# Complex-decay attention before an expert layer: time moves from the free axis to the partitions

## The chip, the cores and the metric

One Trainium2 chip, one of its cores. The metric is the device time of one execution in microseconds (us), from launch to end. A profiled execution of the same program tells where the time goes; it has its own time, given below.

## What is computed

Three layers follow one another: an attention with a complex decay per channel, a mixture of 8 experts where each token goes to one, and a dense layer with a gated nonlinearity. The change is in the first. Its reference, cut to what matters:

```python
mag = np.sqrt(a_re * a_re + a_im * a_im)
scale = np.minimum(mag, 0.999) / (mag + 1e-06)
a_re_n, a_im_n = a_re * scale, a_im * scale
for t in range(S):                       # S = 768 steps, 4 batches, 8 heads, D = 48
    new_re = ar * S_re - ai * S_im
    new_im = ar * S_im + ai * S_re
    kv = np.einsum('bhd,bhe->bhde', k[:, :, t], v[:, :, t])
    S_re, S_im = new_re + kv, new_im
    y[:, :, t] = np.einsum('bhd,bhde->bhe', q[:, :, t], S_re)
```

The kernels don't step through time. They take the logarithm of the decay's size and its angle, sum both along time, and turn them into factors for q and k, so that a chunk of 128 steps becomes matrix products: scores (k by q), a causal mask, scores by v, and a state that is carried from chunk to chunk.

## The kernel before, in words

The attention works on units of one to three chunks of 128 steps of one batch (`UNITS`, 10 units, 24 chunks). All is fp32. In each unit the decays, q and k lie with (head, channel) on the partitions and time along the free axis: 384 channels are 128 partitions by 3 columns of time (`pack`, `row_order`). A unit (`unit`) takes these steps:

- VectorE clamps `ar` (L399), ScalarE takes its logarithm and reciprocal (L400, L401), `ai` is multiplied by the latter (L402), VectorE squares it (L409), ScalarE takes the arctangent (L417).
- **Sums along time** are VectorE scans: the angle (L421, with a carry from the unit before) and the logarithm (L460, begun anew in each chunk). The angle is brought into one turn by L427 (ScalarE) and L431 (VectorE), the last column is kept as the carry (L433).
- ScalarE makes sine, cosine and the growing and falling exponentials; six products of q and k with them follow (`times`, L473), each on VectorE or GpSimd.
- **The move.** The rows of q and k belong to the heads in a packed order, and a matrix product wants one head's real and imaginary part on 112 partitions of one tile `z`. Ten SBUF-to-SBUF transfers per unit on SyncE's queue put them there (`remap`, L348).

A chunk (`chunk`) then has, on TensorE, the scores (L534), two groups of transposes of k (L517), the attended values (L561) and the products for the state (L571); VectorE masks the scores (L542) and carries the state (L575, L581); ScalarE copies what was transposed (L524) and the result `xT` (L600). `Router.steps` follows: a projection (L729), two ScalarE passes (L735, L787) and a score of tiny VectorE instructions (L740 to L814) that route the tokens. When all chunks are done, `Router.blocks` orders the tokens by expert, rows are gathered (`r<-xd`), and the expert layer begins with a transpose (`px`, L1062).

**What sets the order.** Nothing of this order stands in the code as written. `Plan` holds every step as a node with an engine (or a choice of two), a cost in ns, what it reads and writes, and the number of buffers of each tile; `Plan.order` lists them greedily by due time, `Plan.run` tries 600 disturbed due times and emits the best list. It also inserts spare matmuls into TensorE's waits (`busy`, L148). Each engine then runs its list strictly in order. The plan's cost of a scan of 384 columns is 130 + 1.0417 · 384 = 530 ns, and it lets VectorE and GpSimd run side by side at no cost.

Of the kernel before, what the change touches and what calls it, by code (L numbers as in the profile page):

```python
# [69 lines left out]
def const_arrays():  # L70
    t = np.arange(P)
    ca = np.zeros((P, P + W), np.float32)
    ca[:, :P] = t[:, None] <= t[None, :]
    ca[:, P:] = np.arange(W) % P != 0
# [44 lines left out]
def row_order():  # L119

    o = np.zeros((P, NK, 2), np.int64)
    for p in range(96):
        for kc in range(NK):
            o[p, kc] = (2 * kc + p // 48, p % 48)
    for p in range(96, 128):
        o[p, 0] = (6, p - 96)
        o[p, 1] = (7, p - 96)
        o[p, 2] = (6, 32 + p - 96) if p < 112 else (7, 32 + p - 112)
    return o


def slot(h):
    return h if h >= 6 else 3 * (h % 2) + h // 2


def pack(a):

    o = row_order()
    return np.ascontiguousarray(a[:, o[..., 0], :, o[..., 1]].transpose(2, 0, 1, 3))
# [11 lines left out]
class Plan:  # L151

    LAG, OWN, LOAD = 250, 200, 1283
# [8 lines left out]
    def add(s, engs, cost, fn, r=(), w=(), new=(), due=math.inf, table=None, late=0):  # L164
# [4 lines left out]
        n.warm = getattr(fn, "warm", None)  # L169
        n.deps = set()  # L170
# [23 lines left out]
    def order(s, seek, switch, phase=0.0):  # L194
# [4 lines left out]
        ticks = {}  # L199
        opened = {t: [] for t in s.bufs}  # L200
# [39 lines left out]
        while ready:  # L240
            can = []
            low = inf, inf, None
            for n, o in ready.items():
                t = start(n) if n.new else 0
                if t == inf:
                    continue
                due = n.due + switch if n.table and n.table != table else n.due
                for e, cost, r in o:
                    b = max(t, r, free.get(e, 0))
                    can.append((due, n.id, b, e, n, cost))  # L250
                    if (b, due) < low[:2]:
                        low = b, due, e
# [8 lines left out]
            fill, t = 0, b + cost  # L261
            if e == "PE":
# [49 lines left out]
def attention(tc, ctx, cst, ca, qk, v, ar, ai, rt, psr, wkr, chores, last):  # L312

    nc = tc.nc
    N = len(UNITS)
    T = {}
    plan = Plan({"ar": 3, "ai": 3, "t1": 2, "t2": 2, "t3": 2, "qk": 2, "o": 1, "ar_": 1, "ai_": 1, "t1_": 1, "t2_": 2, "t3_": 1,
                 "qk_": 1, "o_": 1, "v": 2, "carry": 2, "kt": 1, "sT": 2, "st": 2, "pt": 2, "ps": 2, "py": 1, "ds": 1, "xT": 1,
                 "pr": 2, "row": 2, "lg": 2, "s": 2, "u": 3, "si": 2, "ws": 9}, free=("t2", "t2_"))
    add = plan.add  # L320
    with ExitStack() as right, ExitStack() as left:
# [4 lines left out]
        wk = left.enter_context(tc.tile_pool(name="a_wk", bufs=2))  # L326
        pst = left.enter_context(tc.tile_pool(name="a_pst", bufs=2, space=PSUM))
# [9 lines left out]
        def packed(k, n, room, top):  # L337

            t = tile_(room, [P, 2 * NK * top * (P + 1)], k)
            T[k] = t[:, :2 * NK * n * (P + 1)].rearrange("p (q k n) -> p q k n", q=2, k=NK)  # L340
            return T[k]

        def remap(z, src, r0):

            for dst, s in ((z[r0:r0 + 48, :, 0:3], src[0:48]), (z[r0:r0 + 48, :, 3:6], src[48:96]),
                           (z[r0:r0 + 32, :, 6:8], src[96:128, :, 0:2]), (z[r0 + 32:r0 + 48, :, 6:7], src[96:112, :, 2:3]),
                           (z[r0 + 32:r0 + 48, :, 7:8], src[112:128, :, 2:3])):
                nc.sync.dma_start(dst.rearrange("p q k n -> p q (k n)"), s.rearrange("p q k n -> p q (k n)"))  # L348

        zs = [zp.tile([DP, 2 * H * (W + U)], F32, tag=f"z{i}", name=f"z{i}") for i in range(2)]  # L350
        cp = left.enter_context(tc.tile_pool(name="a_cst", bufs=1))
        end = left.enter_context(tc.tile_pool(name="a_end", bufs=1))
        a = cp.tile([P, P + W], F32, name="ca")
        caus, begin = a[:, :P], a[:, P:]
        for i in range(2):
            add("Pool", 5200, lambda i=i: nc.gpsimd.memset(zs[i][32:64], 0.0), w=[("z", i, 0), ("z", i, 1)])

        def unit(u):

            b, c0, n = UNITS[u]  # L360
            w = n * P
            e = NK * w
            ts = slice(c0 * P, (c0 + n) * P)
# [3 lines left out]
            AR, AI, T1, T3, QK, O = ((t + mark, u) for t in ("ar", "ai", "t1", "t3", "qk", "o"))  # L367
            TE, TD = ("t2" + mark, 2 * u), ("t2" + mark, 2 * u + 1)
            VV = ("v", u)
            ar3, ai3 = ([(*k, i) for i in range(NK)] for k in (AR, AI))  # L370
# [4 lines left out]
            def x(k):  # L375
                return T[k][:, :, :w]

            def new(k):
                return tile_(room, [P, NK, top * P], k)[:, :, :w]

            def load(k, src):
                def f():
                    nc.sync.dma_start(new(k), src[b, :, :, ts])
                return f

            def loadqk():
                nc.sync.dma_start(packed(QK, n, room, top)[:, :, :, :w], qk[b, :, :, ts].rearrange("p (q k) t -> p q k t", q=2))
# [6 lines left out]
            if u == 0:  # L394
                add("SP", 728, lambda: nc.sync.dma_start(a, ca), w=["ca"], late=2000)
            add("SP", 2.84 * e, loadqk, w=q3 + k3 + [(*QK, "e")], new=[QK], late=2000)
            add("SP", 1.42 * e, loadv, w=[VV], new=[VV], late=2000)

            add("DVE", fast, lambda: V.tensor_scalar(out=x(AR), in0=x(AR), scalar1=1e-5, scalar2=None, op0=ALU.max), w=ar3)  # L399
            add("ACT", actc, lambda: act(x(AR), x(AR), AF.Ln), w=ar3, table=LNEXP)  # L400
            add("ACT", actc, lambda: act(new(T1), x(AR), AF.Exp, scale=-1.0), r=ar3, w=[T1], new=[T1], table=LNEXP)  # L401
            add(both, 0, lambda g: engines[g].tensor_tensor(out=x(AI), in0=x(AI), in1=x(T1), op=ALU.mult), r=[T1], w=ai3)  # L402

            def tan2():
                if n == U:
                    i, o = (T[k].rearrange("p k t -> p (k t)") for k in (AI, T1))
                else:
                    i, o = x(AI), x(T1)
                V.tensor_tensor_reduce(out=o, in0=i, in1=i, scale=1.0, scalar=0.0, op0=ALU.mult, op1=ALU.max,  # L409
                                       accum_out=cst["rmax"][:, u:u + 1])  # L410

            add("DVE", full, tan2, r=ai3, w=[T1, ("rmax", u)])
# [6 lines left out]
            def total(i):  # L419
                def f():  # L420
                    V.tensor_tensor_scan(out=x(AI)[:, i], data0=cst["one"].to_broadcast([P, w]), data1=x(AI)[:, i],  # L421
                                         initial=T["carry", u - 1][:, i:i + 1] if c0 else 0.0, op0=ALU.mult, op1=ALU.add)
                return f

            for i in range(NK):
                add("DVE", 130 + 1.0417 * w, total(i), r=[("carry", u - 1)] if c0 else [], w=[(*AI, i)])
            add("ACT", actc + 94, lambda: act(new(T3).bitcast(I32), x(AI), AF.Identity, scale=1 / (2 * math.pi)),  # L427
                r=ai3, w=[T3], new=[T3])

            def rest():  # L430
                V.scalar_tensor_tensor(out=x(AI), in0=x(T3).bitcast(I32), scalar=-2 * math.pi, in1=x(AI), op0=ALU.mult, op1=ALU.add)  # L431
                if c0 + n < NC:
                    V.tensor_copy(tile_(wk, [P, NK], ("carry", u)), x(AI)[:, :, w - 1])  # L433

            k = [("carry", u)] if c0 + n < NC else []
            add("DVE", full + 200 * len(k), rest, r=[T3], w=ai3 + k, new=k)
# [1228 lines left out]
```

## Time and profile before

| | us |
|---|---|
| median of 3 runs | 986.34 (984.12 to 989.18) |
| profiled execution, its own time | 984.68 |
| its span, first to last instruction | 982.9 |
| TensorE busy | 844.6 (86%) |
| VectorE busy | 665.8 (68%) |
| ScalarE busy | 518.6 (53%) |
| GpSimd busy | 313.1 (32%) |

The shares are means over three layers with different limits. The attention with its routing takes the first third of the span; the two dense layers after it are the same instructions in both kernels. In the profile PE is TensorE's matrix products, PEld its weight loads, DVE VectorE, ACT ScalarE, POOL GpSimd, SP SyncE; a q behind the name is the engine's queue. One fp32 matrix product shows as two PE records, one transpose as one.

### The profile page before, as it was taken

To read this page: it belongs to the slowest core of one execution; us is meant where nothing else is said; L and a number is where in the kernel's file an instruction comes from. 1 tells how busy PE (TensorE), PEld (TensorE's weight loads), DVE (VectorE), ACT (ScalarE), POOL (GpSimd) and SP (SyncE) were. 2 spreads that over 40 slices of the span, in tenths; PEclk is the share of its full clock that TensorE was granted. 3 is DMA by queue.
4 is the path that set the end of the run, shared out by engine and by line. 5 is a ranking of instruction groups with operands and counts; after the bars stand their busy time and mean duration, and the time that the engine had idled before them with its cause. 6 is when DMAs were issued, how large, how long until landed. Compare 5 with 4: busy or idle time off the path is not lost.

```text
span 982.9 us, 17388 instructions
## 1 busy us (share of the span) xinstructions
PE 844.6 (86%) x5994; PEld 561.3 (57%) x5994; DVE 665.8 (68%) x1367; ACT 518.6 (53%) x987; POOL 313.1 (32%) x253
## 2 busy tenths in 40 slices
PE   0567687578786899998899999999999999999994
PEld 0567686568685566655556654444655545556662
DVE  7999998999776799988999659998045071250000
ACT  6756667667655576774773347676054172340000
POOL 7546252634421674451550112331320100001110
PEclk9777787888896999999999999999999999999998
DMA  8589867697674574663656432330110000000000
GB/s 264 147 194 210 147 169 178 110 204 140 123 233 152 163 199 154 197 188 122 181 174 207 149 121 62 93 97 1 49 49 9 25 1 17 17 2 25 27 30 19
DMA packets 58020, 114.15 MB, mean 116 GB/s; under 512 B 7521, under 2 KB 36834, under 8 KB 57922
## 3 DMA queue, kind: packets, MB, share of 16 engines
q1 hardware_dynamic: 52754, 97.02, 37.7%
q0 software_dynamic: 4736, 14.69, 4.9%
q8 instruction: 56, 0.92, 0.4%
q10 hardware_dynamic: 432, 1.18, 0.4%
q14 instruction: 42, 0.34, 0.1%
HBM read 75.04 MB, written 18.81 MB: 95 GB/s over the span
## 4 chain that ended last, share of the span: by engine, by line
PE 45%; DVE 12%; DMA 3%; issue 3%; ACT 3%; POOL 0%; POOLq 0%; DVEq 0%; ACTq 0%
PE fpo L1303 18%; PE fph L1283 11%; PE py L1099 6%; PE ph L1074 4%; PE ph L1075 2%; DVE w L955 2%; DMA wh<-w 2%; DVE x L1287 2%; DVE acc L1106 1%; PE pt L1084 1%; DVE h L1078 1%; DVE hT L1088 1%; PE px L1062 1%; DVE w L958 1%; ACT h L1077 1%
## 5 line engine op out<-in xcount | busy, mean ns | idle before, releaser
L1283 PE MATMUL fph<-fx,fw 128*128 128x512 f16 x864 | 192.2, 379 | 5.6 <-DVE x L1287 5.6
L1287 DVE SCALAR_TENSOR_TENSOR x<-fph,x 128x512 f32<-128x512 f32 x96 | 65.9, 688 | 129.8 <-ACT x L1286 128.2
L1283 PEld LDWEIGHTS <-fw 128*128 128x128 f16 x864 | 84.4, 98 | 104.3 <-issue 8.8
L1303 PE MATMUL fpo<-fw,gT 128*128 128x384 f16 x768 | 125.3, 326 | 0.0
L1099 PE MATMUL py<-w,hT 128*128 x624 | 118.0, 326 | 1.2
L1074 PE MATMUL ph<-w,x 128*128 x312 | 107.5, 379 | 1.8 <-ACT x L1063 0.9
L534 PE MATMUL ps<-z 112*128 112x128 f32 x384 | 68.7, 337 | 44.0 <-DMA z<-qk 37.8
L1303 PEld LDWEIGHTS <-gT 128*128 128x128 f16 x768 | 75.1, 98 | 49.9
L1307 ACT ACTIVATE x<-fpo,fsm 128x384 f32<-128x384 f32 x24 | 13.9, 580 | 167.5 <-PE fpo L1303 167.5
L1308 POOL DMA_INDIRECT out<-x,fto x24 | 23.2, 965 | 245.4 <-ACT x L1307 245.4
L994 POOL TENSOR_TENSOR w<-ws,w 128x768 f16<-128x768 f32 x40 | 68.6, 1716 | 83.3 <-ACT w L993 79.1
L1286 ACT ACTIVATE x<-fph,fsm 128x512 f32<-128x512 f32 x96 | 65.5, 684 | 49.1 <-PE fph L1283 36.2
L534 PEld LDWEIGHTS ps<-z 112*128 112x128 f32 x384 | 60.8, 242 | 49.1 <-DMA z<-qk 27.7
L1075 PE MATMUL ph<-w,x 128*128 x312 | 84.9, 272 | 1.6 <-DVE x L1064 1.5
L1099 PEld LDWEIGHTS <-hT 128*128 128x128 f16 x624 | 60.9, 98 | 32.4 <-issue 3.6
L1077 ACT COPY h<-ph 128x256 f32<-128x256 f32 x104 | 38.4, 369 | 57.0 <-PE ph L1075 50.3
L1303 PE MATMUL fpo<-fw,x 128*128 128x384 f16 x384 | 62.7, 326 | 0.0
L1078 DVE TENSOR_TENSOR h<-ph,h 128x256 f32<-128x256 f32 x104 | 43.5, 418 | 26.9 <-ACT h L1077 21.6
L1303 PEld LDWEIGHTS <-x 128*128 128x128 f16 x384 | 37.6, 98 | 25.0
L561 PE MATMUL py<-z,st 112*48 112x128 f32 (+1 forms) x320 | 38.0, 320 | 13.0 <-DVE st L581 6.6
L1106 DVE SCALAR_TENSOR_TENSOR acc<-py,rs,acc 128x384 f32<-128x384 f32 x78 | 47.6, 610 | 1.4 <-PE pt L1084 0.6
L1074 PEld LDWEIGHTS <-x 128*128 128x128 f16 x312 | 30.5, 98 | 31.0 <-ACT x L1063 1.6
(239 smaller groups left out, 1735.6 us busy)
## 6 DMA issues: line engine op xcount, KB each, us to landing
ws<-in_we SPq DMA_DIRECT2D x61, 384.0 KB
w<-in_w SPq DMA_DIRECT2D x32, 384.0 KB
qk<-in_qk SPq DMA_DIRECT2D x6, 1152.0 KB
z<-o SPq DMA_DIRECT2D x12, 435.4 KB
z<-qk SPq DMA_DIRECT2D x12, 435.4 KB
yd<-acc SPq DMA_DIRECT2D x26, 192.5 KB
xd<-row SPq DMA_DIRECT2D x6, 589.5 KB
ar<-in_ar SPq DMA_DIRECT2D x6, 576.0 KB
```

Of the source, the lines that this page charges most:

```text
L534: nc.tensor.matmul(ps[:, h - 4 * i, :], lhsT=T["z", u][:, 1, slot(h), ts], rhs=T["z", u][:, 0, slot(h), ts], start=True, stop=True)
L994: nc.gpsimd.tensor_tensor(out=wv[:, :, 1, :], in0=sv, in1=wv[:, :, 0, :], op=ALU.subtract)
L1074: nc.tensor.matmul(ph, lhsT=xT[:, b - lo, 0, k, :], rhs=w[:, e, o:o + 2 * FQ], start=k == 0, stop=False)
L1075: nc.tensor.matmul(ph[:, :FQ], lhsT=xT[:, b - lo, 1, k, :], rhs=w[:, e, o:o + FQ], start=False, stop=k == KD - 1)
L1077: nc.scalar.copy(h, ph[:, FQ:])
L1078: nc.vector.tensor_tensor(out=h, in0=ph[:, :FQ], in1=h, op=ALU.add)
L1099: nc.tensor.matmul(py, lhsT=hT[:, hl, j, :], rhs=w[:, e, o + off:o + off + DM], start=i == 0, stop=i == n - 1)
L1106: nc.vector.scalar_tensor_tensor(out=a, in0=py, scalar=s, in1=a, op0=ALU.mult, op1=ALU.add)
L1283: nc.tensor.matmul(ph, lhsT=s.wi[f][:, a, k, :], rhs=xT[b][:, k], start=i == 0, stop=i == 3 * KD - 1)
L1286: nc.scalar.activation(h, ph, AF.Sigmoid, scale=sig)
L1287: nc.vector.scalar_tensor_tensor(out=h, in0=ph, scalar=GS, in1=h, op0=ALU.mult, op1=ALU.mult)
L1303: nc.tensor.matmul(po, lhsT=gT[:, f, a, g * P:(g + 1) * P], rhs=s.wo[f][:, b, :], start=i == 0, stop=i == 3 * s.NF - 1)
```

## The change

Time goes onto the partitions, channels onto the free axis. A chunk of `ar`, `ai`, q, k is a tile of 128 steps by 384 channels (`by_time`), all heads side by side.

- The sums along time are matrix products with a triangle of ones (`caus`): `total` in `phases` (angle, L401, plus L403 which adds the last row of the chunk before by a weight tile that is one on partition 127) and in `logs` (logarithm, L447). They land in PSUM (`sc`, two banks), from where ScalarE and VectorE read, chunk by chunk: L406, L409, L450, L455. The scans, the carry and L433 are gone.
- The products with sine and cosine write one tile `f` (`turn` in `unit`, L491) in which the 48 real and 48 imaginary channels of a head lie side by side. The `z` tiles, their zeroing on GpSimd (L356), `ends` (L479) and `remap` are gone.
- Per chunk, 16 transposes on TensorE (L517: 8 heads, q and k, also in a batch's last chunk, where before there were 8 transposes of k and none in the last chunk) turn `f` into `zq` and `zk`, and four copies of 96x512 bring them from PSUM, on ScalarE or VectorE (L525). The scores (L535) read these. The state's products (L569) read `f` as it lies, 8 instead of 16 per chunk.
- The decay over a chunk, which before was a column, is now a row: two transfers per unit (`whole`, L464), one small transpose (L467) and a copy (L472) turn it.
- The routing tile `pr` has one PSUM buffer instead of two; the scores share three banks with the transposes.
- `Plan` learns of a shared port: a VectorE or GpSimd node marked `port` isn't begun while a marked one of the other engine runs.

The core of the diff:

```diff
+        n.port = port or getattr(fn, "port", False)
...
+        pair = {"DVE": ("Pool", 0), "Pool": ("DVE", 0)}
...
                     b = max(t, r, free.get(e, 0))
+                    if n.port and e in pair and pair[e][1] > b:
+                        b = pair[e][1]
...
+            if n.port and e in pair:
+                pair[pair[e][0]] = e, t
...
-            def total(i):
-                def f():
-                    V.tensor_tensor_scan(out=x(AI)[:, i], data0=cst["one"].to_broadcast([P, w]), data1=x(AI)[:, i],
-                                         initial=T["carry", u - 1][:, i:i + 1] if c0 else 0.0, op0=ALU.mult, op1=ALU.add)
-                return f
...
+                def total():
+                    if j == 0:
+                        new(T3)
+                    ps = tile_(psc, [P, 512], S)[:, :DM]
+                    nc.tensor.matmul(ps, lhsT=caus, rhs=xj(AI, j), start=True, stop=before is None)
+                    if before:
+                        nc.tensor.matmul(ps, lhsT=tail, rhs=xj(before[:2], before[2]), start=False, stop=True)
...
+                def rest():
+                    V.scalar_tensor_tensor(out=xj(AI, j), in0=xj(T3, j).bitcast(I32), scalar=-2 * math.pi, in1=T[S][:, :DM],
+                                           op0=ALU.mult, op1=ALU.add)
...
-            for i in range(NK):
-                add("DVE", 69 + 1.0417 * w, logs(i), r=["ca"], w=[(*AR, i)])
...
+                    nc.tensor.matmul(tile_(psc, [P, 512], S)[:, :DM], lhsT=caus, rhs=xj(AR, j), start=True, stop=True)
...
-            add("SP", 600 + 3.2 * e, place(0), r=[(*O, 0), (*O, 1), (*O, "e")], w=[("z", u % 2, 0)], late=2000)
-            add("SP", 600 + 3.2 * e, place(1), r=q3 + k3 + [(*QK, "e")], w=[("z", u % 2, 1)], late=2000)
+                for i, f, r in ((0, T3, t33), (1, SN, [SN])):
+                    add(both, 0, turn(k, i, f), r=r + s + [(*FF, 0, 0)] * (k + i > 0), w=[(*FF, k, i)], new=[] if k + i else [FF], port=True)
...
+                    pt = turning(4 * g + 2 * i + k)
                     for h in range(4):
-                        nc.tensor.transpose(pt[:, h, :], T["z", u][:, 1, slot(4 * i + h), ts], cst["ident"][:DP, :DP])
+                        nc.tensor.transpose(pt[:2 * D, h, :], T[FF][:, k, j * H + 4 * i + h].rearrange("p i d -> p (i d)"), cst["ident"])
...
+                    add({"ACT": 480, "DVE": 602}, 0, turned(k, i), r=[("pt", m)] + [(*z, 0)] * i, w=[(*z, i)], new=[] if i else [z])
```

How the lists of the engines change, at three places.

TensorE, around the fourth chunk of the first batch (`ps` or `pt` scores, `z` the moved q and k, `c` the identity, `py` the attended values). Before:

```order
L729 MATMUL pr_662<-wg,xT_652 128x104 x4
L148 MATMUL ps_678<-c_60 128x128
L534 MATMUL ps_678<-z_125 128x128 x4
L534 MATMUL ps_685<-z_125 128x128 x4
L517 MATMUL pt_694<-c_60,z_125 128x112 x4
L517 MATMUL pt_704<-c_60,z_125 128x112 x4
L534 MATMUL ps_716<-z_125 128x128 x4
L561 MATMUL py_727<-z_125,st_673 64x128
```

The same chunk with the change (`f` the products with sine and cosine, `sc` the sums along time, `ca` the triangle):

```order
L127 MATMUL pt_671<-c_60 128x128 x5
L517 MATMUL pt_671<-c_60,f_635 96x128 x4
L517 MATMUL pt_686<-c_60,f_635 96x128 x4
L517 MATMUL pt_693<-c_60,f_635 96x128 x4
L401 MATMUL sc_700<-ai_242,ca 128x384
L403 MATMUL sc_700<-ai_242,c_60 128x384
L535 MATMUL pt_708<-zq_664,zk_691 128x128 x4
L535 MATMUL pt_714<-zq_664,zk_691 128x128 x4
L733 MATMUL pr_725<-wg,xT_643 128x104 x4
L517 MATMUL pt_730<-c_60,f_635 96x128 x4
L517 MATMUL pt_738<-c_60,f_635 96x128 x4
L569 MATMUL ds_743<-v_408,f_635 96x48 x8
```

The scores no longer wait for a transfer into `z`; they stand behind 16 transposes and, in TensorE's own list, behind the sums of a later unit.

VectorE, in the middle of the second batch. Before, a scan, the mask and the reduction of the angle by whole units:

```order
L799 SCALAR_TENSOR_TENSOR lg_1110<-row_1119,c_60 128x24
L460 SCALAR_TENSOR_TENSOR ar_655<-ca,ar_655 128x384
L542 TENSOR_TENSOR sT_1317<-ps_1290,ca 128x512
L801 TENSOR_REDUCE s_1120<-lg_1110 128x3
L431 SCALAR_TENSOR_TENSOR ai_746<-t_5_1272,ai_746 128x1152
L433 COPY carry_1326<-ai_746 128x3
```

With the change, at the end of the first batch:

```order
L438 SCALAR_TENSOR_TENSOR ar__9_229<-ar__9_229,t__18_788 128x384
L525 COPY zq_857<-pt_901 96x512
L789 TENSOR_SCALAR u_906<-u_906 128x1
L793 TENSOR_SCALAR row_889<-u_906 128x1
L525 COPY zk_867<-pt_912 96x512
L542 TENSOR_TENSOR sT_936<-pt_919,ca 128x512
L573 TENSOR_TENSOR st_943<-ds_927,st_782 96x384
L579 TENSOR_TENSOR st_943<-st_943,mb_651 96x384
L542 TENSOR_TENSOR sT_936<-pt_938,ca 128x512
L486 TENSOR_TENSOR qk_436<-qk_436,t_7_846 128x1152
L486 TENSOR_TENSOR qk_436<-qk_436,ar_265 128x1152
L491 TENSOR_TENSOR f_997<-qk_436,t_3_646 128x24x48
```

The scans are out; copies out of PSUM and more of the products of q and k have come in. Over the stage VectorE's list has 42 of the 96 copies L525; GpSimd's has 28 of the products L378, L486 and L491 (16 of 1152 columns, 6 of 768, 6 of 384), where it had 41 of L402 and L473 (27, 8, 6).

SyncE's queue in the first batch. Before:

```order
L383 DMA ai_497<-in_ai 128x3x384
L348 DMA z_125<-o_465 48x2x1161 x2
L348 DMA z_125<-o_465 32x2x774
L348 DMA z_125<-o_465 16x2x387 x2
L348 DMA z_125<-qk_335 48x2x1161 x2
L348 DMA z_125<-qk_335 32x2x774
L348 DMA z_125<-qk_335 16x2x387 x2
L383 DMA ar_655<-in_ar 128x3x384
```

With the change:

```order
L363 DMA qk_436<-in_qk 128x2x1152
L808 DMA xd<-row_417 128x393
L464 DMA mt_574<-t_5_522 24x1x48 x2
L358 DMA ai_637<-in_ai 128x1152
L366 DMA v_649<-in_v 128x1152
L358 DMA ar_661<-in_ar 128x1152
```

Ten large transfers per unit have become two of one row.

## Rows read from the trace of the kernel before

**Rows 1.** Busy us (instructions) per engine in stretches of the span, clock, DMA.
```profile
core 0: us, PE busy (x) PEld busy (x) DVE busy (x) ACT busy (x) POOL busy (x), PEclk, DMA share, GB/s
0.00:318.00 318.00, 213.62 (x2349) 199.50 (x2349) 275.60 (x543) 204.59 (x298) 144.34 (x92) 0.83 0.75 175
...
125.00:150.00 25.00, 21.58 (x286) 20.41 (x285) 23.99 (x51) 18.42 (x28) 13.98 (x7) 0.90 0.61 150
...
175.00:200.00 25.00, 14.60 (x153) 13.10 (x154) 23.70 (x42) 18.14 (x23) 16.64 (x9) 0.77 0.74 110
```

**Rows 2.** The chain that ended last, around the stage's end: start us, us, what.
```profile
317.85 3.94 DMA r<-xd,gidx
```

**Rows 3.** Waits up to 318 us: engine, line, waited for: us, times, longest.
```profile
PE ps L534 <- DMA z<-qk: 37.8, 13, 6.4
PE ps L148 <- POOL o L473: 28.7, 1, 28.7
...
SPq L387 <- DMA z<-qk: 33.7, 13, 8.1
```

**Rows 4.** Groups of DVE up to 318 us: count, busy us, mean ns, idle before.
```profile
L542 DVE TENSOR_TENSOR sT<-ps,ca 128x512 f32<-128x512 f32 x48 | 32.8, 683 | 14.9 <-PE ps L534 14.8
L460 DVE TENSOR_TENSOR_SCAN ar<-ca,ar 128x384 f32<-128x384 f32 (+2 forms) x27 | 30.1, 1137 | 0.0
L421 DVE TENSOR_TENSOR_SCAN ai<-c,carry,ai 128x384 f32<-128x384 f32 (+1 forms) x15 | 18.3, 1260 | 0.0
...
L431 DVE SCALAR_TENSOR_TENSOR ai<-t,ai 128x1152 f32<-128x1152 int32 (+2 forms) x9 | 10.5, 1162 | 0.0
L421 DVE TENSOR_TENSOR_SCAN ai<-c,ai 128x384 f32<-128x384 f32 (+1 forms) x12 | 9.7, 815 | 0.0
```

**Rows 5.** Groups of DVE by form, the same columns; the last from the expert layer.
```profile
L473 DVE TENSOR_TENSOR qk<-qk,ai 128x1152 f32<-128x1152 f32 x6 | 8.1, 1350 | 0.0
...
L797 DVE TENSOR_TENSOR row<-lg,s 128x24 f32<-128x24 f32 x6 | 6.0, 992 | 0.0
...
L809 DVE TENSOR_TENSOR lg<-pr,oh 128x24 f32<-128x24 f32 x6 | 1.0, 172 | 0.3
...
L1106 DVE SCALAR_TENSOR_TENSOR acc<-py,rs,acc 128x384 f32<-128x384 f32 x78 | 47.6, 610 | 1.4 <-PE pt L1084 0.6
```

**Rows 6.** Timelines of POOL and DVE near 98 us: start us, us, instruction.
```profile
97.39 2.84 POOL L473 TENSOR_TENSOR qk<-qk,ai 128x1152 f32<-128x1152 f32 x1
...
97.93 2.33 DVE L799 SCALAR_TENSOR_TENSOR lg<-row,c 128x16 f32<-128x16 f32 x1
```

**Rows 7.** Groups of ACT up to 318 us; then its first arctangent in the timeline.
```profile
L306 ACT ACT_TABLE_LOAD x26 | 33.4, 1283 | 1.2 <-PEq L1655 0.7
L524 ACT COPY kt<-pt 128x448 f32<-128x448 f32 x40 | 20.8, 528 | 20.4 <-PE pt L517 19.4 <-PE ds L571 1.0
L600 ACT COPY xT<-py 112x512 f32<-112x512 f32 x24 | 14.0, 582 | 14.5 <-PE py L561 14.4
...
L735 ACT ACTIVATE row<-pr 128x384 f32<-128x384 f32 x24 | 11.7, 489 | 21.0 <-DVE lg L740 18.2 <-PE pr L729 2.8
...
L427 ACT ACTIVATE t<-ai 128x1152 int32<-128x1152 f32 (+2 forms) x9 | 9.2, 1018 | 6.1 <-DVE ai L421 6.1
...
15.35 0.62 ACT L417 ACTIVATE ai<-ai,rok 128x384 f32<-128x384 f32 x1
```

**Rows 8.** Timeline of PE: bursts of scores and transposes, and what follows them.
```profile
68.78 2.07 PE L534 MATMUL ps<-z 112*128 112x128 f32 x8 [4.37 <-DVE sT L542]
...
258.55 1.96 PE L534 MATMUL ps<-z 112*128 112x128 f32 x16
260.35 1.04 PE L729 MATMUL pr<-wg,xT 112*128 112x104 f32 x8
...
288.79 0.98 PE L517 MATMUL pt<-c,z 112*128 112x112 f32 x8
289.61 1.05 PE L729 MATMUL pr<-wg,xT 112*128 112x104 f32 x8
```

More of the change, by code (lines that the diff above doesn't have):

```diff
@@ L116, in f64_layout, with by_time @@
     return np.ascontiguousarray(np.concatenate([a, b], 0)).view(np.int64)
[L119 to L139, printed above, removed]
+def by_time(a):
+    return a.reshape(B, H, NC, P, D).transpose(0, 3, 2, 1, 4).reshape(B, P, NC, DM)
 SEED, TRIES, SPREAD = 11, 600, 400
@@ L162, in __init__, with add @@
         s.nodes, s.writer, s.readers, s.uses, s.opened = [], {}, {}, {}, {}
-    def add(s, engs, cost, fn, r=(), w=(), new=(), due=math.inf, table=None, late=0):
+    def add(s, engs, cost, fn, r=(), w=(), new=(), due=math.inf, table=None, late=0, port=False):
         n = type("Node", (), {"prev": None})()
@@ L437, in size @@
+            for j in range(n):
+                phases(j)
             def size(eng):
@@ new lines, in unit, with whole, turned @@
+            for j in range(n):
+                logs(j)
+            def whole():
+                m = tile_(wk, [U * H, 2, D], MT)
+                for i in range(2):
+                    nc.sync.dma_start(m[:n * H, i, :], x(TD)[P - 1:P, :])
+            def turned():
+                nc.tensor.transpose(tile_(psc, [P, 512], ("sc", 1000 + u))[:2 * D, :n * H],
+                                    T[MT][:n * H].rearrange("p i d -> p (i d)"), cst["ident"][:n * H, :n * H])
+            add("SP", 400, whole, r=td3, w=[MT], new=[MT], late=2000)
@@ new lines, in unit, with factors @@
+            add("PE", 60, turned, r=[MT], w=[("sc", 1000 + u)], new=[("sc", 1000 + u)])
+            add("ACT", 120, lambda: nc.scalar.copy(tile_(wk, [2 * D, U * H], MB)[:, :n * H], T["sc", 1000 + u][:2 * D, :n * H]),
+                r=[("sc", 1000 + u)], w=[MB], new=[MB])
+            add("DVE", 78, lambda: V.tensor_reduce(out=cst["emin"][:2 * D, u:u + 1], in_=T[MB][:, :n * H], axis=AX.X, op=ALU.min),
+                r=[MB], w=[("emin", u)])
+            def factors():
+                return T.get(FF) or tile_(zp, [P, 2, U * H, 2, D], FF)
@@ L581, in state @@
                 V.tensor_tensor(out=sv, in0=sv if c else T[PD].rearrange("p (h d) -> p h d", h=H), in1=mb, op=ALU.mult)
-            if not final:
-                for i in range(2):
-                    t = add("PE", 384, turn(i), r=Z, w=[("pt", 2 * g + i)], new=[("pt", 2 * g + i)])
-                    t.warm = lambda n, i=2 * g + i: busy(nc, turning(i)[:, 0, :], cst["ident"], n)
-                    add("ACT", 424, turned(i), r=[("pt", 2 * g + i)] + [(*KT, 0)] * i, w=[(*KT, i)], new=[] if i else [KT])
@@ L590, in chunk @@
+            for i in range(2):
+                S = ("pt", 10000 + 2 * g + i)
                 first = g + i == 0
                 if first:
[L592 to L594 removed]
+                    add("PE", COLD * 430, lambda: busy(nc, scores(0)[:, 0, :], cst["ident"], COLD), r=[("f", 0, 0, 0)], w=[S], new=[S])
+                s = add("PE", 890, score(i), r=[(*ZQ, i), (*ZK, i)], w=[S], new=[] if first else [S])
```

243 lines of the change are left out of this document (111 added, 132 removed).

## The prediction

> **What bounds the kernel now.** I first asked the chain of waits where the attention ends: the rows for the expert layer are fetched at 317.85 us [rows 2]. All the change touches lies before that; the 665 us behind it are the same instructions and only shift. So the question is how long the first 318 us become. The busy time by stretches [rows 1] says what fills them: DVE 275.6 us, PE 213.6, ACT 204.6, POOL 144.3. DVE is the fullest and leaves 42.4 us open. Its waits are few, 14.8 us for scores [rows 4]; it is late, others wait for it. PE's waits are of another kind [rows 3]: 28.7 us until the first factors exist, 37.8 us for the transfers into `z`. They cost little today, because DVE would be late anyway, but they hold PE's granted clock at 0.83 over the stage: 0.90 where PE is busy 21.6 of 25 us, 0.77 where it is busy 14.6 [rows 1]. DVE's time has two parts that the change aims at. The scans: 54 of the 60 take 30.1 + 18.3 + 9.7 = 58.1 us [rows 4], 1.1 to 1.3 us each by the larger groups, where the plan believed 0.53. And standstill: a 16-column instruction that reads SBUF twice took 2.33 us, begun at 97.93 while a GpSimd product ran from 97.39 to 100.23; it ended at 100.26, with that product [rows 6]. L797 takes 992 ns, L809, the same shape but with one input in PSUM, 172 ns [rows 5].
>
> **VectorE, part by part.** Out: scans, -58.1. In: 42 copies of 96x512 out of PSUM. The trace has no such copy; between ACT's 582 ns for 512 columns [rows 7] and the masks' 683 ns, which read PSUM and write 512 columns on DVE [rows 4], I take the masks', nearest in engine and size: +28.7 (24.4 at the low end). Products that left GpSimd: eleven of 1152 columns at 1350 ns [rows 5] and two of 768 at two thirds of that: +14.9 + 1.8 = +16.7. The reduction of the angle becomes 24 pieces of 384 columns that read PSUM: at L1106's 610 ns [rows 5], the same operation on 384 columns of PSUM, 14.6 instead of 10.5 [rows 4]: +4.1. Without relief from the standstill DVE comes to 275.6 - 58.1 + 28.7 + 16.7 + 4.1 = 267.0. **Relief:** GpSimd has 28 products instead of 41, no zeroing, no `ends`, and the plan now keeps marked pairs apart. Four tiny lines like L797 have ten instructions each; if all lose 0.82 us (992 - 172), that is 33 us. Only two of the four are marked, so I take half, 16; the ends are 0 (the order drifts on the chip and the pairs meet anyway) and 33. **DVE: 251 us**, 234 to 267.
>
> **TensorE.** Scores at clock 1.00: 16 records in 260.35 - 258.55 = 1.80 us [rows 8], so an fp32 product of 128 columns (two records) 0.225 us, one of 384 columns 0.675. The sums are 24 + 20 + 24 = 68 of these: +45.9. Transposes: 8 in 289.61 - 288.79 = 0.82 us [rows 8], 0.1025 each over 112 columns, 0.117 over 128; 384 of them +45.0, the old 160 -16.4. Spare matmuls fall from 81 to 45 in the lists: -8.1. The state's products halve in number but stream as much; nothing for them. Net +66.4 us at full clock. Today's work at full clock is 213.6 · 0.83 = 177 us, so PE comes to **244 us at full clock**; that is an upper value, since a burst's last record counts its drain as busy. At clock c it takes 244/c. A busier PE than in the 0.90 window [rows 1] should be granted more; I take 0.93: 262 us.
>
> **ScalarE.** 40 copies go, -20.8; 54 of 96x512 come at 582 ns, +31.4; four more table loads, +5.1; 72 short passes over PSUM at 489 ns instead of three times 9.2 us, +7.6 [rows 7]. 204.6 + 23.3 = 228 us. No longer idle cover, but below the other two.
>
> **Queues and buffers.** SP loses 100 transfers and gains 20 of one row. These wait for an exponential, and the loads of later units stand behind them on SP; but before, loads stood behind `z` for 33.7 us [rows 3], so I cost this at nothing. If that cover fails, `ai` comes late and PE's sums, early in its list, hold the scores behind them. `pr` with one bank makes each projection wait for the ACT pass of the one before; a chunk takes some 12 us (318/24), two passes take 1.1 [rows 7], so nothing until the last chunks. `f` must not be overwritten before the last products; nothing.
>
> **The sum.** DVE: 251 plus the 42 us that it leaves open today is 293. PE is the new bound: its first work needs only the first arctangent, which ends at 15.97 us [rows 7], instead of 28.7 [rows 3]. Of today's idle, 318 - 213.6 - 28.7 - 37.8 = 37.9 us have other causes (states, masks, the routing chain at the end); the longer list gives PE something else to do in part of them. Between 0 and 38 I take half, 19. 16 + 262 + 19 = **297 us for the stage instead of 318, -21**. On the profiled execution's 984.68 that gives 963.7; the median of the runs lies 1.7 us above that execution, so I predict **965 us**.
>
> **A rule against it.** One transpose record lasts 0.98 - 7 · 0.1025 = 0.26 us, but the next begins after 0.1025 [rows 8]; the sum goes by the second. The Trainium skill, in "TensorE: Matmul & The Clock Gate", section "Part 4: PE-mode transpose", gives about 275 ns for one 128x128 transpose inside a kernel (bf16). By that figure 384 of them take 105.6 us, the stage would end near 297 + 60.6/0.93 = 362 us and the kernel near 1030. The trace agrees with it as a length and not as a distance, so it gets little below.
>
> **Rivals.**
> - *PE is full and still waits* (0.14). All 37.9 us stay, because three engines of 228 to 262 us now wait for one another through three `pt` and two `sc` banks: 16 + 262 + 38 = 316, kernel 984. For it: each chunk crosses PE and a copying engine six times. Against: the plan's list keeps several units in flight.
> - *The drains vanish and the ports stay clear* (0.13). PE packs without gaps at clock 1.00, with 10 us of waits (all but the routing at the end): 16 + 244 + 10 = 270, kernel 938. DVE at its low end, 234, fits in that.
> - *Slower: the clock* (0.16). PE is now the bound, and half clock doubles its work: 8 records took 2.07 us at 68.78 us where 16 took 1.96 later [rows 8]. Every wait of the kind that gave 0.77 [rows 1] then costs on the path. If the clock stays at today's 0.83: 16 + 294 + 19 = 329, kernel 997. It decides at 244/c + 35 = 318, c = 0.86: below that the change loses. Against: the largest single cause of PE's waits, `z`, is gone.
> - *Slower: transposes cost their length* (0.02). At 0.26 us each, interleaved too thinly to overlap: +55/0.93, kernel 1024. Against it are the bursts of eight [rows 8].
> - *The plan's port rule does nothing on the chip.* Then DVE is 267, plus 42 is 309: a 9 us gain. This lies inside the forecast's own range.
>
> **How the numbers follow.** The forecast has 0.55, with its own range 950 to 978 (stage 282 to 310: waits and clock each off by half). What a measurement here can tell from no change is 0.5%, 4.9 us: 981.4 to 991.3. Faster: 0.55 + 0.13 = 0.68. Same: 0.14, the first rival. Slower: 0.16 + 0.02 = 0.18. The range is 940 to 995: it drops half of the fast rival and somewhat more than half of the slow ones, 0.07 + 0.11.
>
> **What would show it.** Right: the fetch `r<-xd` near 297; PE first busy near 16 us, busy some 260 us to there at a clock of 0.9 or more; no wait for `z`; DVE near 251 with the copies L525 near 0.68; L797's successor (L801) well under 992 ns; 384-column products about 0.68 apart. Wrong: DVE still the longest in the stage (ports), PE's clock under 0.86, waits of PE for ACT or DVE copies beyond some 40 us, or a later layer that changes by more than a few us, which I hold fixed.

## The result and the profile after

The changed kernel takes 970.08 us (median of three runs; 968.65 to 971.64), the kernel before 985.23 (984.02 to 989.18) on the same chip: a ratio of 0.9845, 95% interval 0.9819 to 0.9871, or 15 us less. A fourth run of the changed kernel was a slow one, 1549.21 us at a granted clock of 0.56, and is left out of these figures. The forecast was 965 with 940 to 995, and faster. The profiled execution took 970.08 us, its span is 968.3.

The chain of waits of the changed kernel, start, length and what, at the end of the stage:

```profile
301.37 4.05 DMA r<-xd,gidx
305.46 0.92 PE px L1067 x3
```

The fetch is at 301.37 instead of 317.85 [rows 2], 16.5 us earlier; what follows it gives 1.8 us back (968.3 - 301.4 = 666.9 against 982.9 - 317.85 = 665.1), so the gain lies in the attention, as forecast. The first transposes `px` of the expert layer took 0.92 us here, and 0.56 before. The granted clock around them, in the kernel before and in the changed one:

```profile
320.00:325.00 5.00, 2.99 (x16) 1.76 (x15) 2.71 (x4) 0.74 (x2) 4.04 (x4) 0.88 0.46 128
303.00:308.00 5.00, 2.88 (x12) 1.73 (x11) 3.22 (x5) 0.48 (x1) 3.83 (x4) 0.50 0.44 116
```

The changed kernel enters the expert layer at 0.50, the lower of the clock's two levels (1.2 of 2.4 GHz), where the kernel before had 0.88. TensorE had sat idle for 4.2 us just before its last spare products (the third line of the waits below), against 1.6 us before.

Busy time by stretches of the changed kernel; the columns are those of [rows 1]:

```profile
0.00:301.40 301.40, 258.94 (x2327) 219.24 (x2328) 240.93 (x552) 222.56 (x368) 79.14 (x52) 0.95 0.36 121
50.00:250.00 200.00, 186.59 (x1746) 159.41 (x1745) 171.21 (x366) 151.39 (x252) 55.92 (x22) 0.97 0.26 86
250.00:304.00 54.00, 42.11 (x409) 37.92 (x406) 41.14 (x134) 30.57 (x55) 15.26 (x12) 0.84 0.42 146
304.00:968.00 664.00, 630.82 (x3635) 361.06 (x3634) 387.97 (x822) 314.26 (x689) 166.52 (x161) 0.99 0.28 88
```

TensorE is now the fullest engine, 258.9 us at a granted clock of 0.95, where it had 213.6 at 0.83 [rows 1]; VectorE fell from 275.6 to 240.9, GpSimd from 144 to 79, the DMA share from 0.75 to 0.36. Between 50 and 250 us TensorE is idle for 13 of 200 us.

TensorE's longest waits in the stage, in the columns of [rows 3]:

```profile
PE sc L401 <- ACT ai L389: 13.0, 2, 11.9
PE pr L753 <- DVE oh L806: 5.0, 3, 2.2
PE hot L127 <- DVEq L1574: 4.2, 1, 4.2
PE sc L401 <- DVE ai L409: 4.1, 2, 3.3
PE pr L733 <- DVE lg L813: 2.5, 2, 1.9
```

The 37.8 us for `z` and the 28.7 for the first factors [rows 3] are gone; the first sum starts at 11.88, when the first arctangent is done.

Groups of VectorE by form, in the columns of [rows 4]:

```profile
L542 DVE TENSOR_TENSOR sT<-pt,ca 128x512 f32<-128x512 f32 x48 | 32.9, 685 | 6.5 <-PE pt L535 5.8
L579 DVE TENSOR_TENSOR st<-st,mb 96x384 f32<-96x384 f32 x16 | 16.4, 1026 | 0.0
...
L525 DVE COPY zk<-pt 96x512 f32<-96x512 f32 x21 | 14.3, 681 | 5.8 <-PE pt L517 5.4
L525 DVE COPY zq<-pt 96x512 f32<-96x512 f32 x21 | 14.3, 681 | 3.6 <-PE pt L517 3.5
...
L409 DVE SCALAR_TENSOR_TENSOR ai<-t,sc 128x384 f32<-128x384 int32 x23 | 12.5, 545 | 2.2 <-ACT t L406 2.0
...
L803 DVE SCALAR_TENSOR_TENSOR lg<-row,c 128x16 f32<-128x16 f32 x2 | 2.7, 1374 | 0.0
...
L801 DVE TENSOR_TENSOR row<-lg,s 128x24 f32<-128x24 f32 x6 | 1.1, 176 | 0.0
```

L801, which the plan now keeps clear of GpSimd, takes 176 ns where L797 took 992 [rows 5]. L803, which isn't marked, still stands still at times, 1374 ns for 16 columns. So does the state, L579, though marked: 1026 ns, and the shortest of the sixteen takes 542.

For the whole stage I summed up, over all VectorE instructions up to the fetch, the time of each above the shortest of its line, tiles and form; below this is called the **standstill**. It is 68 us in the kernel before, 15 of them in the scans, and 30 in the changed one (62.7 and 30.6 in the expectations below, from a slightly different grouping of forms).

### The profile page after: what moved, and what is told of

The parts are those of the page before. It is cut to its first block, busy times and chain, and to the rows that moved or that the text cites. A ratio compares the mean times of both kernels' runs of the same rounds, so it can differ in the third digit from the quotient of the medians.

```text
span 968.3 us, 17226 instructions
## 1 busy us (share of the span) xinstructions
PE 892.4 (92%) x5972; PEld 582.7 (60%) x5972; DVE 631.5 (65%) x1376; ACT 536.8 (55%) x1057; POOL 248.0 (26%) x213
## 4 chain that ended last, share of the span: by engine, by line
PE 44%; DVE 14%; DMA 4%; issue 3%; ACT 2%; POOL 0%; ACTq 0%; POOLq 0%; DVEq 0%; SPq 0%
PE fpo L1308 19%; PE fph L1288 12%; PE py L1104 5%; PE ph L1079 4%; DVE w L960 2%; DMA wh<-w 2%; PE ph L1080 2%; DVE acc L1111 2%; DVE x L1292 2%; DVE h L1083 1%; PE pt L1089 1%; DVE hT L1093 1%; DVE w L966 1%; DVE w L963 1%; PE px L1067 1%
## 5 line engine op out<-in xcount | busy, mean ns | idle before, releaser
L1079 PE MATMUL ph<-w,x 128*128 x312 | 108.9, 383 | 1.1 <-ACT x L1068 0.8
L1080 PE MATMUL ph<-w,x 128*128 x312 | 85.7, 275 | 1.8 <-DVE x L1069 1.6
L1308 PE MATMUL fpo<-fw,x 128*128 128x384 f16 x384 | 62.7, 326 | 0.0
L517 PE MATMUL pt<-c,f 128*96 128x128 f32 x384 | 53.9, 280 | 4.0 <-DVE u L747 1.9
L517 PEld LDWEIGHTS pt<-c,f 128*96 128x96 f32 x384 | 43.2, 130 | 14.5 <-issue 6.5
L535 PE MATMUL pt<-zq,zk 96*128 96x128 f32 x384 | 51.4, 283 | 0.0
L1079 PEld LDWEIGHTS <-x 128*128 128x128 f16 x312 | 30.8, 99 | 31.3 <-ACT x L1068 1.6
L535 PEld LDWEIGHTS pt<-zq,zk 96*128 96x128 f32 x384 | 47.5, 196 | 2.0 <-ACT zk L525 0.6
```

What stands on the lines that cost most here:

```text
L517: nc.tensor.transpose(pt[:2 * D, h, :], T[FF][:, k, j * H + 4 * i + h].rearrange("p i d -> p (i d)"), cst["ident"])
L535: nc.tensor.matmul(ps[:, h - 4 * i, :], lhsT=T[ZK][:, h, :], rhs=T[ZQ][:, h, :], start=True, stop=True)
L1079: nc.tensor.matmul(ph, lhsT=xT[:, b - lo, 0, k, :], rhs=w[:, e, o:o + 2 * FQ], start=k == 0, stop=False)
L1080: nc.tensor.matmul(ph[:, :FQ], lhsT=xT[:, b - lo, 1, k, :], rhs=w[:, e, o:o + FQ], start=False, stop=k == KD - 1)
L1308: nc.tensor.matmul(po, lhsT=gT[:, f, a, g * P:(g + 1) * P], rhs=s.wo[f][:, b, :], start=i == 0, stop=i == 3 * s.NF - 1)
```

## The experiments

Differences to the changed kernel are differences of the ratios to the kernel before, times 985 us; with the intervals of both ratios each is uncertain by 3 to 4.5 us. "Fetch" is the start of `r<-xd` in the run's profile, to be held against 301.4 (changed) and 317.9 (before).

### What bounds the stage now: more work on one engine at a time

The order on every engine is that of the changed kernel in these four runs. Run pe_more:

```diff
                     ps = scores(2 * g + i)
+                    busy(nc, ps[:, 0, :], cst["ident"], 2)
```

> The changed kernel with two spare products ahead of each of the 48 groups of scores, in the same order on every engine; 96 x 0.225 = 21.6 us of TensorE work, the output unchanged. My theory (TensorE bounds the stage; between 50 and 250 us it is busy 45 to 48 of every 50 us at a clock of 0.97 or more): nearly all of it is paid, 971 becomes 989 to 994, and the last fetch moves from 301 to 319 to 324. Rival 1 (three engines wait for one another, none bounds): a third, 975 to 981. Rival 2 (the extra work falls into TensorE's idle 43 us): 970 to 974, TensorE's waits shrink by some 20 us.

Measured: ratio 0.9929 (0.9901 to 0.9957), +8.3 us; the fetch at 309.7. The stretch from 50 to 250 us of this run:

```profile
50.00:250.00 200.00, 191.92 (x1814) 166.32 (x1812) 160.39 (x357) 151.30 (x249) 50.77 (x20) 0.98 0.25 86
```

TensorE got busier, 191.9 instead of 186.6 of 200 us, and its clock stood at 0.98. Of 21.6 us some 11 went into its idle time up to 300 us (300 - 269.8 against 300 - 258.8). So "TensorE bounds" fell: 0.38 us was paid for each us of work.

Run dve_more (`g` counts the chunks):

```diff
-                    V.tensor_tensor(out=T["sT", g][:, 4 * i:4 * i + 4, :], ...
+                    for _ in range(1 + (i or g % 3 == 0)):
+                        V.tensor_tensor(out=T["sT", g][:, 4 * i:4 * i + 4, :], ...
```

> The changed kernel with 32 of the 48 masks done twice, same order; 32 x 0.685 = 21.9 us of VectorE work, the output unchanged. My theory: VectorE is busy 243.5 of 304 us and has room, but a second mask also stands in the path from scores to attended values: 0 to +8 us, 971 to 979. Rival 1 (engines balanced): +6 to +9. Rival 2 (VectorE still bounds, as before the change): +18 to +22, 989 to 993. The order of the three answers (TensorE, VectorE, ScalarE) is what tells.

Measured: 0.9895 (0.9863 to 0.9927), +4.9 us, the fetch at 309.8, 8.4 later: 0.2 to 0.4 for each us.

Run act_more:

```diff
+                for _ in range(3):
-            ... nc.scalar.copy(tile_(wkr, [DP, 4, P], ("xT", g)), T[PY])
+                    nc.scalar.copy(o, T[PY])
```

> The changed kernel with each copy of a chunk's result out of PSUM done three times, same order; 48 x 0.585 = 28.1 us of ScalarE work, the output unchanged. My theory: ScalarE is busy 222.6 of 304 us; only the last chunk's two extra copies lie on the path, 1.2 us, and some of the copies that TensorE waits for come later: +1 to +8, 972 to 979. Rival (balanced): +9. Rival (ScalarE is the hidden bound through the copies that scores wait for): +20 or more, 991 and up.

Measured: 0.9954 (0.9935 to 0.9973), +10.7 us, the fetch at 314.0, 12.6 later: 0.38 to 0.45 for each of 28.1 us, on the engine that I took for the freest of the three.

Run pe_less:

```diff
-                    nc.tensor.matmul(ps, lhsT=caus, rhs=xj(AI, j), start=True, stop=before is None)
-                    if before:
-                        nc.tensor.matmul(ps, lhsT=tail, rhs=xj(before[:2], before[2]), start=False, stop=True)
+                    nc.tensor.matmul(ps, lhsT=caus, rhs=xj(AI, j), start=True, stop=True)
```

> The changed kernel without the 20 products that add the last row of the chunk before to the sum of the angle (the carry is left out, so the angles begin anew in each chunk), same order; 20 x 0.675 = 13.5 us of TensorE work less, and the sums no longer wait for the chunk before (4.1 us of waits). My theory (TensorE bounds): 11 to 17 us less, 954 to 960. Rival 1 (balanced): 4 to 6 less, 965 to 967. Rival 2 (another engine or a chain of waits is the bound right below): under 3 less, 968 or more.

This kernel leaves out the carry of the angle from chunk to chunk; the other instructions stay as they are. Measured: 0.9804 (0.9768 to 0.984), -4.0 us, which is within the uncertainty, with the fetch at 301.6, no earlier than in the changed kernel: 0 to 0.3 of each us. The stretch from 50 to 250 us:

```profile
50.00:250.00 200.00, 182.85 (x1686) 158.83 (x1681) 166.98 (x362) 150.18 (x250) 56.90 (x22) 0.93 0.25 86
```

The clock stood at 0.93 here and at 0.97 in the changed kernel. So leaving out 13.5 us of work took only 5 us off TensorE's busy time (258.8 to 253.7 up to 300 us): what was left ran slower.

Together: no engine bounds the stage by itself. Added work on any of the three is paid at 0.2 to 0.45 of its length. My theory fell; its rival 1, three engines that wait for one another, stands. What was added also stands in each chunk's own path from `f` to the routing, so these runs don't tell a fuller engine from a longer path.

### What the parts of the change are worth on the kernel before

Run old_no_scan, in the order of the kernel before:

```diff
-                add("DVE", 130 + 1.0417 * w, total(i), ...
+                add("DVE", 130 + 1.0417 * w, lambda: None, ...
-                add("DVE", 69 + 1.0417 * w, logs(i), ...
+                add("DVE", 69 + 1.0417 * w, lambda: None, ...
```

> The kernel before without its 60 scans (the sums along time are left out), in the same order on every engine: 58.1 us of VectorE work less. Theory 1 (VectorE bounds the stage before; what it loses is gained until TensorE and its waits for z stand in the way): 15 to 25 us less than before, 961 to 971. Theory 2 (engines wait for one another, about a quarter to a third of what one loses is gained, as the four runs on the changed kernel showed): 14 to 19 less. Theory 3 (the transfers into z hold the stage, VectorE only fills the time): under 5 less, 981 or more.

Run old_thin_z, also in that order:

```diff
+            add("Pool", 5200, lambda i=i: nc.gpsimd.memset(zs[i], 0.0), ...
-            add("Pool", 5200, lambda i=i: nc.gpsimd.memset(zs[i][32:64], 0.0), ...
                 nc.sync.dma_start(dst.rearrange(...), s.rearrange(...))
+                break
```

> The kernel before with one of the five transfers in each move into z (the others are left out, z is zero there), in the same order: a fifth of the transfers, two thirds of their bytes gone. Theory 1 (VectorE bounds, z waits cost little, as the prediction had it): 0 to 5 us less than before, TensorE's 37.8 us of waits for z become waits for products. Theory 2 (the transfers are on the path and hold TensorE and its clock): 10 to 25 less, the clock in the stage rises from 0.83 to 0.88 or more.

Both kernels as a whole took 1304 us: the layers behind the attention work on other data and run 335 us longer, so the kernel's time tells nothing and only the fetch is read. It came at **302.1 without the scans (15.7 us earlier)** and at **303.2 with the thin transfers (14.7 earlier)**. For the scans, theories 1 and 2 expected the same and aren't told apart; VectorE's busy time fell by 50 us (275.6 to 225.4). For `z`, theory 1, the prediction's, fell. Two of TensorE's waits in the kernel before:

```profile
PE py L561 <- DVE st L581: 6.6, 5, 3.1
PE ps L534 <- DVE sT L542: 4.4, 1, 4.4
```

and its longest waits in old_thin_z:

```profile
PE ps L148 <- POOL o L474: 28.7, 1, 28.7
PE ps L535 <- DVE sT L543: 17.6, 4, 6.7
PE py L562 <- DVE st L582: 14.2, 8, 5.5
PE ps L535 <- DVE u L744: 8.6, 1, 8.6
...
PE ps L535 <- DMA z<-qk: 4.8, 1, 4.8
```

The waits for `z` shrank from 37.8 to 4.8 us, and nearly all of it came back as waits for VectorE (masks, states and L744), as theory 1 had it. The stage ended 14.7 us earlier all the same, and the busy time to the fetch says where the time went:

```profile
0.00:303.20 303.20, 201.94 (x2349) 188.00 (x2349) 277.13 (x543) 203.88 (x298) 143.28 (x92) 0.87 0.50 145
```

The same 2349 TensorE instructions were busy for 201.9 us at a clock of 0.87, where they took 213.6 at 0.83 [rows 1]: 11.7 of the 14.7 us are TensorE's own work running faster; its idle time fell by 3 us only (104.2 to 101.3). Without the scans it is the same picture: 202.7 us at 0.87. I had priced a wait by whether another engine would be late anyway, and put no price on the clock beside it. Why the clock rose while TensorE was idle for nearly as long, in fewer and longer waits, is not shown; nor is it that the faster products, and not some other effect of the emptier queue, brought the fetch forward.

Run old_rule: the rule in `Plan.order` as in the change, `port=True` on the same operations of the kernel before, layout unchanged.

```diff
+                    if n.port and e in pair and pair[e][1] > b:
+                        b = pair[e][1]
...
-            add(both, 0, times(QK, None, 0, TD), r=[TD], w=q3)
+            add(both, 0, times(QK, None, 0, TD), r=[TD], w=q3, port=True)
```

> The kernel before with the plan's port rule and the marks on the same operations, layout unchanged; the plan draws a new order. Theory 1 (VectorE's standstill on the port, 62.7 us over the shortest durations of each form, is halved and a quarter to a third of that is gained): 7 to 12 us less than before, 974 to 979. Rival 1 (the rule is the whole gain of the change): 13 to 16 less, 970 to 973. Rival 2 (engines are kept apart by waiting, nothing is gained): within 3 us of before; VectorE's busy time falls, its idle time grows.

Measured: 1.0132 (1.0088 to 1.0176), **13 us slower**, outside all three. The standstill fell as expected, from 68 to 35 us, and VectorE's busy time up to 300 us from 264 to 239; but the fetch came at 321.0, 3 us later, and TensorE waited longer for the transfers:

```profile
PE ps L540 <- DMA z<-qk: 47.2, 15, 6.7
```

So far this is rival 2: what no longer stands still waits instead. The other 8 us lie behind the fetch (994.1 - 321.0 = 673.1 against 665.1); where they come from stays open. It is a single draw of the order; two draws by the same rule lay 12.5 us apart with the new layout (below), so this run doesn't show that the rule as such costs 13 us here.

### The port rule with the new layout

Run new_no_rule:

```diff
-        n.port = port or getattr(fn, "port", False)
+        n.port = False
```

> The changed kernel with the plan's port rule switched off; the plan draws a new order. VectorE's standstill over the shortest durations of each form is 30.6 us with the rule. Theory 1 (a quarter to a third is paid): standstill 45 to 60, 3 to 9 us more than the changed kernel, 974 to 980. Rival 1 (the rule is the whole gain): 983 to 987. Rival 2 (the rule does nothing, GpSimd has few products left to meet): 968 to 973, standstill within 5 us of 30.6.

Measured: 1.0053 (1.0027 to 1.0079), **+20.5 us**; the fetch at 313.1, the standstill 44 us. All of the gain in the kernel's time was gone; of the stage's 16.5 us, 4.7 were left. Two draws of a random search stood behind this difference, so the next two runs took another seed. Run seed12:

```diff
-SEED, TRIES, SPREAD = 11, 600, 400
+SEED, TRIES, SPREAD = 12, 600, 400
```

> The changed kernel with another seed of the plan's random search (12 for 11), nothing else. It measures how far two orders drawn by the same rule lie apart. Theory 1 (the order is good by the rule, not by luck): within 4 us of the changed kernel, 967 to 975. Rival (the changed kernel's order is a lucky draw): 976 to 985, and then neither the kernel without the rule nor the kernel before with it says anything of the rule.

Measured: 0.9718 (0.9692 to 0.9744), 958.39 us, **-12.5 us**, which neither theory had: the changed kernel's order was no lucky draw but the worse of two. Run no_rule12, both edits:

> The changed kernel without the port rule, drawn with seed 12. Theory 1 (the rule is worth what the run without it showed with seed 11, where the fetch came at 313 instead of 301): 8 to 18 us above the run with seed 12 and the rule, 979 to 989, VectorE's standstill above 40 us. Rival (that run was an unlucky draw): within 4 us of the run with the rule.

Measured: 1.0005 (0.9989 to 1.0022), 28 us above seed12. The same stretch with the rule, seed12:

```profile
50.00:250.00 200.00, 190.21 (x1814) 164.49 (x1813) 165.37 (x376) 164.78 (x274) 72.95 (x31) 0.99 0.32 105
```

and without it, no_rule12:

```profile
50.00:250.00 200.00, 180.74 (x1625) 152.55 (x1623) 179.45 (x343) 147.09 (x244) 69.86 (x28) 0.95 0.25 85
```

Without the rule VectorE is busy for 14 us more and gets 33 instructions less done, TensorE 189 less. What it spends the time on stands in its timeline and GpSimd's (start, length, what) in no_rule12:

```profile
128.56 3.74 POOL L378 TENSOR_TENSOR ai<-ai,t 128x1152 f32<-128x1152 f32 x1
132.26 3.74 POOL L491 TENSOR_TENSOR f<-qk,sn 128x1152 f32<-128x1152 f32 x1
...
129.75 0.68 DVE L542 TENSOR_TENSOR sT<-pt,ca 128x512 f32<-128x512 f32 x1
130.35 0.14 DVE L793 TENSOR_SCALAR row<-u 128x1 int32<-128x1 int32 x1
130.41 3.11 DVE L491 TENSOR_TENSOR f<-qk,sn 128x1152 f32<-128x1152 f32 x1
133.44 0.68 DVE L542 TENSOR_TENSOR sT<-pt,ca 128x512 f32<-128x512 f32 x1
134.04 3.17 DVE L491 TENSOR_TENSOR f<-qk,t 128x1152 f32<-128x1152 f32 x1
```

Two products of 1152 columns took 3.11 and 3.17 us on VectorE where 1.34 is the shortest, beside products on GpSimd that took 3.74 each where 2.62 is; the masks between them, one input in PSUM, kept their 0.68. The rows show the two engines taking turns. The GpSimd product L378 ended at 132.30, the VectorE product begun at 130.41 ended at 133.52, 1.22 us later; the next pair ended at 136.00 and 137.21, 1.21 apart. Each VectorE product thus waited for the GpSimd product to end and then took nearly its whole 1.34. All 28 instructions of VectorE that were held over 0.3 us in this run ran beside a GpSimd instruction, and so did all 18 in the changed kernel, where 139 of VectorE's 552 instructions did. The Trainium skill, in "SBUF — State Buffer", section "Who interferes with whom", says that VectorE instructions with two SBUF inputs contend with GpSimd's reads and those with at most one (outside VectorE's two-port modes) don't. These rows agree.

Standstill and fetch of the six kernels of the new layout without added work (the last two from the section below):

| run | standstill, us | instructions held over 0.3 us | fetch, us |
|---|---|---|---|
| seed12 | 15.1 | 9 | 286.8 |
| tail_bridge | 27.9 | 17 | 297.7 |
| the changed kernel | 29.6 | 18 | 301.4 |
| best12 | 31.0 | 18 | 302.1 |
| new_no_rule | 43.7 | 28 | 313.1 |
| no_rule12 | 45.9 | 28 | 316.0 |

From the first to the last, 30.8 us of standstill go with 29.2 us of stage, 0.95 for each, far above the 0.2 to 0.45 that a us of even work costs. Part of it is the clock, 0.99 against 0.95 in the two stretches above. That the rest comes from standstill striking single links of the chains (L801, L812, the state) and GpSimd at once is argued, not shown; the orders also differ in other things.

### The tail, and a better version

Run tail_bridge, same order (`heat` writes to a `ds` tile; the spare products of `AWAKE` just before go there too):

```diff
-            busy(nc, T[CNT][:, P:2 * P], cst["ident"], BRIDGE)
+            heat(BRIDGE)
```

> The changed kernel with the spare products at the end of the routing written to another PSUM bank than the one from which the gathered rows' numbers are read; same order on every engine. In the changed kernel this read waits 2.8 us for the spare products. Theory 1 (this wait stands directly ahead of the fetch): the fetch comes 2 to 3 us earlier, 968 to 969. Rival (the read then waits for something that comes as late): within 1 us of the changed kernel.

Measured: 0.9812 (0.9793 to 0.9831), **-3.3 us**, the fetch at 297.7, 3.6 us earlier. VectorE's timeline in the changed kernel, the wait in brackets:

```profile
294.10 0.18 DVE L899 TENSOR_TENSOR sidx<-rw,c 128x24 int32<-128x24 f32 x1
297.04 0.19 DVE L878 TENSOR_SCALAR gidx<-pr_cnt 128x32 int32<-128x32 f32 x1 [2.77 <-PE pr_cnt L127]
```

and in tail_bridge:

```profile
293.28 0.18 DVE L905 TENSOR_TENSOR sidx<-rw,c 128x24 int32<-128x24 f32 x1
293.48 0.19 DVE L884 TENSOR_SCALAR gidx<-pr_cnt 128x32 int32<-128x32 f32 x1
```

Theory 1 holds. The change had put the spare products into the tile that this read needs, and so gave back 3 us; I had counted the one bank fewer for `pr` and overlooked this.

Run best12: the bank of tail_bridge, and (with some twenty costs like the last)

```diff
+        if c == NCH - 1:
+            PR, psum = ("sc", 2000), spare or psum
...
-        add("DVE", 73, lambda: V.tensor_tensor(out=self.total, ...
+        add("DVE", 73, shared(lambda: V.tensor_tensor(out=self.total, ...
...
-                    add({"ACT": 480, "DVE": 602}, 0, turned(k, i), ...
+                    add({"ACT": 584, "DVE": 681}, 0, turned(k, i), ...
```

> The changed kernel with the spare products in another bank, the last chunk's projection in a bank of the sums (so that it doesn't wait for the group before), three more port marks in the routing, and the plan's costs of VectorE, ScalarE and GpSimd passes set to the durations that the trace of the changed kernel shows; the plan draws a new order, seed 12. Theory 1 (the engines wait for one another, so an order drawn from true durations waits less): 4.5 us from the two changes of banks and 3 to 8 from the order, 958 to 964. Rival 1 (the order drifts on the chip anyway, only the banks count): 965 to 968. Rival 2 (the draw is worse): 972 or more.

Measured: 0.9906 (0.9876 to 0.9936), 977.61 us, +6.0, and 18.5 us above seed12: rival 2. In this one draw true durations in the plan didn't make the order better; the standstill is 31 us, as in the changed kernel, and 673.9 us follow the fetch, as many as in old_rule. The best version run is seed12, 958.39 us, 2.8% under the kernel before and 1.3% under the changed one. Its read of `gidx` also waits 2.76 us for the spare products, so seed12 with the bank of tail_bridge should come near 955, an estimate; that wasn't run.

## Why the prediction was right, and where it wasn't

The time was 5 us above the forecast, inside both ranges. The sum of the stage, term by term, forecast against trace: first work of TensorE 16 against 11.9; its busy time 262 at clock 0.93 against 258.9 at 0.95; other idle time 19 against 30.6 (301.4 - 11.9 - 258.9); together 297 against 301.4. Then the later layers, 1.8 us. The main sizes held as well: the copies L525 at 681 ns (683 taken), ScalarE 222.6 (228), products of 384 columns 0.65 us apart (0.68), and 12 transposes, begun at 264.99, 1.45 us before what followed, 0.12 each:

```profile
264.99 1.51 PE L517 MATMUL pt<-c,f 128*96 128x128 f32 x12
266.44 0.22 PE L467 MATMUL sc<-c,mt 16*96 16x16 f32 x1
```

There the distance decided and not the length, which is 280 ns in the mean of L517's records. The Trainium skill gives about 275 ns ("TensorE: Matmul & The Clock Gate", "Part 4: PE-mode transpose", for bf16); the trace agrees with that as a length.

What failed are reasons for the gain, and the sum came out right in part by luck: TensorE's early start and fuller clock (7 us less than forecast) and its longer idle time (12 us more) nearly cancelled.

- **"PE is the new bound."** It is the fullest engine, but 21.6 us more cost 8.3, and 13.5 us less brought 4, within the uncertainty, and nothing at the fetch. The idle time beside it, 31 us where half of 38 was taken, is that of a ring of three engines: the first rival's mechanism ("PE is full and still waits") is what the runs show, at a smaller price.
- **"The plan's port rule does nothing on the chip", a gain of 9 us.** The rule does a good deal: with it the standstill is 15 and 30 us with two seeds, without it 46 and 44. Without it the stage ends 2 and 5 us earlier than before, and the kernel gains nothing (ratios of 1.0005 and 1.0053). The term "relief", 16 us between 0 and 33, was somewhat small. The standstill fell by 38 us, but 15 of these lay in the scans and are in their 58.1 us; the other 23 stand against the 16, and VectorE was busy for 240.9 us where I had 251. The four tiny lines (L795, L797, L799, L802) alone fell from 22 to 3.5 us, and five long passes over the decays (L399, L409, L440, L451, L455), which the prediction left out, from 15 to 2; the state and the last products of q and k were held longer than before. And its price was wrong: I let VectorE end at 293 beside TensorE's 297, where a us of VectorE counts for next to nothing, and over six orders a us of standstill went with nearly a us of stage.
- **"They cost little today"**, of the waits for `z`. Thinning the transfers alone brought the fetch 14.7 us forward, dropping the scans alone 15.7; in both TensorE's busy time fell by 11 to 12 us at a higher clock. Either is nearly as much as the 16.5 us of the whole change. With the rule off the stage gains only 2 to 5 us, so the change pays most of either back; that it does so in sums, transposes, copies and standstill is argued, not shown.
- **`pr` with one bank, "nothing until the last chunks".** That held nearly (2.5 us of waits for L813), but the bank taken from the spare products cost 3.3 us at the end.
- The clock rival (0.83, 997 us) did not come: 0.97 from 50 to 250 us.

So the layout alone gains nothing in the kernel's time (two draws), the rule alone on the old layout gained nothing either and was 13 us slower (one draw), and the two together gain 15 us, or 28 with the other seed.

## What to carry to other kernels

When three engines of a pipeline are each 70 to 90% busy, don't take the fullest one for the bound: here added work on any of them counted for 0.2 to 0.45 of its length. Test that by adding work to one engine at a time in an unchanged order. Look in the profile for VectorE instructions of one form whose durations differ by a factor of two or more, and for what runs beside the long ones: here it was a GpSimd instruction each time, and keeping the two apart was worth more than the work that the change moved. Where a random search draws the order, run a second seed before believing a difference of one per cent.

## What the runs showed of the hardware that I had not expected

The attended values stand in TensorE's timeline of the changed kernel in groups of four records (start, length, what):

```profile
216.51 0.39 PE L560 MATMUL py<-zq,st 96*48 96x128 f32 x4
216.74 0.39 PE L560 MATMUL py<-sT,v 128*48 128x128 f32 x4
216.96 0.39 PE L560 MATMUL py<-zq,st 96*48 96x128 f32 x4
```

Four records go into 0.22 us, 0.055 each, where a record of the scores, also 128 columns of fp32, has 0.11 [rows 8]: the products of two heads, whose results go to different partitions of one bank, run side by side. And a meeting on the port holds up both engines in turn: 3.17 us for 1.34 on VectorE beside 3.74 for 2.62 on GpSimd, where the next GpSimd product waits in its turn (2.62 and the 1.22 us that VectorE then took make 3.84).
